# Low halves of the gated products on POOL, and scales of a unit made when both norms are known

## The chip, the cores and the metric

The kernel runs on one core of one Trainium2 chip. The metric is device time in microseconds (us) of one execution. The engines are TensorE (PE in the profile; PEld are its weight loads), VectorE (DVE), ScalarE (ACT), GpSimd (POOL) and SyncE (SP). Each engine executes its own queue of instructions in order and waits on semaphores for the others. SP issues most of the transfers; POOL issues the indirect ones.

## What is computed

Three layers in a row. `attn` is an attention over 32 memory slots for each of 4 batches and 8 heads. Its output, 2304 tokens of 512 numbers, goes through a gated layer, and that through a layer of 8 experts of which each token takes 2.

```python
# attention (4 batches, 8 heads, 576 tokens, 64 numbers, 32 slots)
a = softmax(phi, over tokens)
k_m, v_m = einsum('bhsm,bhsd->bhmd', a, k), einsum('bhsm,bhsd->bhmd', a, v)
x = softmax(q @ k_m.T / 8) @ v_m                 # -> (2304, 512)
# gated layer, d_ff = 1536
x = (sigmoid(x @ w_gate) * (x @ w_val)) @ w_out
# experts: router with noise, top 2 of 8, F = 1024
logits = x @ g + log1p(exp(x @ n)) * noise
for e in range(8):
    out[rows of e] += weight[rows of e] * (relu(x[rows of e] @ w1[e]) @ w2[e])
```

## The kernel before

Products that need more than float16 are made of two halves: a number is scaled and rounded to a float16 high half, the rest becomes a float16 low half, and a product is the sum of high-high, high-low and low-high, three matmuls into one PSUM bank. The helper `split` (L375) does it in two instructions: ScalarE writes the high half (L376), VectorE the low half (L377).

*Weights.* The matrices of the gated layer come as 64-bit patterns in 36 pieces of 512 KB, loaded by SP into four buffers (L318). Each piece is rounded to float32 in four instructions (`rounded`, L325): ScalarE scales the low words (L329), VectorE shifts and joins the high words (L331, L332), POOL adds (L333). POOL's add is the last reader of the piece, so it frees the buffer for the next load. ScalarE then sums the squares (L363 for gate and value weights, L359 for output weights), a matmul with ones (L87) sums them over the partitions, and a few VectorE instructions (L92 to L96) make a power of two and its inverse of it. The generator `weights` walks through the 18 jobs.

*Attention.* For each batch, `memory` makes the slots, `values_scale` their norm, and `attention` the weights of the tokens; POOL multiplies by the inverse sums (L278). The batch's tokens are not multiplied out: `fold` (L231) multiplies the slots into 256 columns of the gate and of the value weights (a unit u of 6) and splits the result into `wq`, with a scale `ws` (L236) made of the unit's and the batch's norms.

*Gated layer, first half.* `stage1` (L410) runs 72 times: 4 batches, 6 units, 3 chunks of 192 tokens. Twenty-four matmuls (L424) fill two PSUM banks, one for the gate and one for the value. Tanh on ScalarE (L427, with a scale `gs` made by VectorE in L388 at first use) gives `sg` in SBUF, from a ring of two buffers; VectorE writes (tanh + 1) times value back into the value's PSUM bank (L429); ScalarE takes the high half out of it (L430) and VectorE the low half (L431). PSUM has a ring of four banks for this (`pg`), which folds, attention and experts share.

*Gated layer, second half.* `stage2` (L433) multiplies 128 tokens with the output weights (L442), `tokens` splits the row and writes it out, `route` finds the two experts, and POOL scatters slot numbers (L586) after copying token numbers (L556).

*Experts.* After the last `stage1` at about 440 us, TensorE runs the experts (L764, L778) to the end; POOL gathers (L749) and scatters (L784) their rows.

*Order.* The program names the instructions in the order of the loops: in the first loop of `build`, a fold, three times a product with three steps of `weights` behind it; later products between the second halves. A planner with priorities then orders each engine's queue and adds the semaphores and the reuse of buffers. The attention of the first batch runs far ahead, that of the later ones somewhat ahead.

Of the kernel before, what the change touches and what calls it, by code (L numbers as in the profile page):

```python
# [26 lines left out]
P = 128  # L27
# [26 lines left out]
SG = 2  # L54
# [12 lines left out]
class Kern:  # L67
# [31 lines left out]
    def consts(self):  # L99
        nc = self.nc  # L100
        cp = self.cp = self.ctx.enter_context(self.tc.tile_pool(name="const", bufs=1, side="left"))
        tmp = ExitStack()
        jp = tmp.enter_context(self.tc.tile_pool(name="tmp", bufs=1, side="right")).tile([P, P], F32, name="jp")
        nc.gpsimd.iota(jp, pattern=[[1, P]], base=0, channel_multiplier=-1, allow_small_or_imprecise_dtypes=True)
        self.idf = cp.tile([P, P], F32, name="idf")
        nc.vector.tensor_scalar(self.idf, jp, 0.0, None, op0=ALU.is_equal)
        self.tri = cp.tile([P, P], F16, name="tri")
        nc.vector.tensor_scalar(self.tri, jp, 0.0, None, op0=ALU.is_gt)
        self.onef = cp.tile([P, P], F32, name="onef")
        nc.vector.memset(self.onef, 1.0)  # L110
        self.ones = cp.tile([P, P], F16, name="ones")
        nc.vector.memset(self.ones, 1.0)
        tmp.close()
# [55 lines left out]
    def memory(self, b, g):  # L169
# [21 lines left out]
        km = a2.tile([P, 2, 2, D], F32, tag="km", name="km")  # L191
# [31 lines left out]
    def values_scale(self, b):  # L223
        m = self.a2.tile([P, 1], F32, tag="vm", name="vm")
        self.xT[b] = self.xp.tile([P, 2, 2, S], F16, tag="x", name="x")
        junk = self.xT[b][:, 0, 0, :P].bitcast(BF16)
        self.nc.scalar.activation(junk, self.flat(self.vbs[b % 2]), AF.Square, accum_out=m)
        self.sv[b], iv = yield from self.norm2(self.cp, m, f"sv{b}", floor=30)
        self.invx.append(iv)

    def fold(self, b, u):  # L231
# [3 lines left out]
        s = self.cp.tile([P, 2], F32, tag="ws", bufs=4, name="ws")  # L235
        nc.vector.tensor_scalar(s, self.sw[u], self.sv[b], 2.0 ** -A_BITS, op0=ALU.mult, op1=ALU.mult)  # L236
# [12 lines left out]
    def attention(self, b):  # L249
# [4 lines left out]
        def scores(u):  # L254
# [15 lines left out]
            ex = a2.tile([P, n, M], F32, tag="ex" if u < 2 else "ex2", name="ex")  # L270
# [24 lines left out]
        self.gs[b] = {}  # L295
# [39 lines left out]
    def weights(self):  # L335
# [6 lines left out]
        def finish(u, wait):  # L342

            s, iv = yield from self.norm2(cp, sums[u], f"w{u}", wait, 2)
            self.sw.append(s)
            self.iwg.append(iv[:, 0:1])
            self.iwv.append(iv[:, 1:2])
            yield
# [36 lines left out]
    def gate_scale(self, b, u):  # L385
        if u not in self.gs[b]:
            g = self.gs[b][u] = self.cp.tile([P, 1], F32, name=f"gs{b}{u}")
            self.nc.vector.tensor_scalar(g, self.iwg[u], self.invx[b], 0.5, op0=ALU.mult, op1=ALU.mult)  # L388
        return self.gs[b][u]
# [20 lines left out]
    def stage1(self, b, u, ch):  # L410
# [16 lines left out]
        nc.scalar.activation(sg, ps[0], AF.Tanh, scale=self.gate_scale(b, u))  # L427
        pv = ps[1]
        nc.vector.scalar_tensor_tensor(pv, sg, 1.0, pv, op0=ALU.add, op1=ALU.mult)  # L429
        nc.scalar.activation(o[:, 0, :, cols], pv, AF.Copy, scale=2.0 ** -16)  # L430
        nc.vector.scalar_tensor_tensor(o[:, 1, :, cols], pv, 2.0 ** -16, o[:, 0, :, cols], op0=ALU.mult, op1=ALU.subtract)  # L431
# [45 lines left out]
    def router_consts(self):  # L477
        nc, a, cp, rz = self.nc, self.a, self.cp, self.rz
        self.ie = cp.tile([P, E], F32, name="ie")
# [417 lines left out]
    def build(self):  # L897
# [6 lines left out]
        self.snapped, self.sv, self.sw, self.wq = False, {}, [], {}  # L904
# [6 lines left out]
        self.xp, self.xT = left(mw, "xp", 2), {}  # L911
        wp = left(mraw, "w1p", 1)
        self.W = [wp.tile([P, KT, 256], F32, name=f"w{i}") for i in range(12)]
        self.gp = right(m1, "gT", GT)
        self.sp = right(m1, "sig", SG)
# [216 lines left out]
```

## Time and profile before

| | |
|---|---|
| time, median of 3 (lowest to highest) | 891.67 us (890.34 to 894.32) |
| time of the profiled execution | 891.72 us |
| its span in the trace | 889.9 us |
| PE busy | 814.8 us (92%) |
| DVE busy | 473.5 us (53%) |
| ACT busy | 456.8 us (51%) |
| POOL busy | 208.6 us (23%) |
| mean granted clock of PE | 0.973 |

The profile is of one execution. A wait "A L1 <- B L2" is time in which engine A stood before its line L1 until engine B had finished its line L2. The granted clock is a share of full speed, 1.0 being 2.4 GHz and 0.5 being 1.2 GHz. Names of tiles are those of the program without numbers.

### The profile page before, as it was taken

How to read it: one execution, taken by the hardware profiler on the slowest of the kernel's cores; microseconds unless marked ns; L12 is line 12 of the kernel's file. 1: busy time of each engine (PE TensorE's matmuls, PEld its weight loads, DVE VectorE, ACT ScalarE, POOL GpSimd, SP SyncE). 2: the span in 40 equal slices, each digit the busy share in tenths (PEclk: the TensorE clock that was granted, in tenths of full speed). 3: DMA queues.
4: the chain of work that ended last, by engine and by line, in shares of the span. 5: the costliest groups of instructions: out<-in, count | busy, mean ns of one | idle time of the engine just before them, and what ended most of it. 6: DMA issues, size and time to landing. Idle time of an engine off the chain costs nothing. (4 is left out here: it accounts for less than half of the span.)

```text
span 889.9 us, 16827 instructions
## 1 busy us (share of the span) xinstructions
PE 814.8 (92%) x6531; PEld 534.0 (60%) x6531; DVE 473.5 (53%) x1317; ACT 456.8 (51%) x907; POOL 208.6 (23%) x210
## 2 busy tenths in 40 slices
PE   5558859999999998898998999999999999999995
PEld 4347746757657765666655656665747556574752
DVE  1788788555647686874443138553444345340110
ACT  3477667615545476672323348564646446461320
POOL 1363440001110201023014443202323122332112
PEclk9998778999999999999999999999999999999998
DMA  9478639324221564546594869826565868473113
GB/s 317 151 258 292 227 115 341 132 75 102 25 78 25 166 214 142 168 166 194 145 346 107 176 132 263 200 95 143 129 188 120 166 141 214 71 117 48 25 13 47
DMA packets 126067, 135.16 MB, mean 152 GB/s; under 512 B 71968, under 2 KB 88480, under 8 KB 125472
## 3 DMA queue, kind: packets, MB, share of 16 engines
q1 hardware_dynamic: 116000, 113.30, 43.9%
q0 software_dynamic: 9984, 20.75, 12.9%
q8 instruction: 52, 0.85, 0.4%
q14 instruction: 31, 0.25, 0.1%
HBM read 87.97 MB, written 30.86 MB: 134 GB/s over the span
## 5 line engine op out<-in xcount | busy, mean ns | idle before, releaser
L424 PE MATMUL pg<-x,wq 128*128 128x192 f16 x1728 | 174.0, 258 | 23.4 <-ACT wq L376 15.1
L424 PEld LDWEIGHTS <-wq 128*128 128x128 f16 x1728 | 152.5, 103 | 44.2 <-ACT wq L376 17.7
L778 PEld LDWEIGHTS <-hT 128*128 128x128 f16 (+1 forms) x960 | 99.8, 105 | 104.8 <-DVE hT L770 0.9
L442 PE MATMUL px<-wo,gT 128*128 128x512 f16 x648 | 148.8, 379 | 0.3 <-issue 0.3
L784 POOL DMA_INDIRECT out<-y,mts x40 | 64.6, 1614 | 208.7 <-ACT y L783 206.9
L778 PE MATMUL py<-w2a,hT 128*128 128x512 f16 (+1 forms) x480 | 105.2, 379 | 0.4 <-DVE hT L770 0.4
L778 PE MATMUL py<-w2b,hT 128*128 128x512 f16 (+1 forms) x480 | 104.9, 379 | 0.0
L764 PE MATMUL ph<-xe,w1a 128*128 128x312 f16 (+2 forms) x768 | 103.3, 296 | 0.0
L770 DVE TENSOR_TENSOR hT<-r,hT 128x312 f16<-128x312 f32 (+2 forms) x128 | 57.4, 480 | 85.9 <-ACT hT L769 84.5
L764 PE MATMUL ph<-xe,w1b 128*128 128x312 f16 (+2 forms) x768 | 103.0, 296 | 0.0
L442 PEld LDWEIGHTS <-gT 128*128 128x128 f16 x648 | 61.5, 98 | 68.6 <-issue 4.5
L783 ACT ACTIVATE y<-py,css 128x512 f32<-128x512 f32 (+1 forms) x40 | 27.5, 687 | 129.6 <-PE py L778 120.6
L764 PEld LDWEIGHTS <-w1b 128*128 128x128 f16 x768 | 75.2, 98 | 27.1
L764 PEld LDWEIGHTS <-w1a 128*128 128x128 f16 x768 | 75.0, 98 | 27.1
L768 ACT ACTIVATE r<-ph 128x312 f32<-128x312 f32 (+2 forms) x128 | 49.7, 428 | 76.5 <-PE ph L764 73.0
L586 POOL DMA_INDIRECT meta<-mt,vi x36 | 36.1, 1003 | 173.8 <-DVE vi L583 46.4
L749 POOL DMA_INDIRECT xg<-xs,mts x40 | 44.4, 1110 | 87.7 <-DMA xe<-xg 49.0
L427 ACT ACTIVATE sg<-pg,gs 128x384 f32<-128x384 f32 x72 | 41.6, 578 | 41.9 <-PE pg L424 27.9
L429 DVE SCALAR_TENSOR_TENSOR pg<-sg,pg 128x384 f32<-128x384 f32 x72 | 40.2, 558 | 36.8 <-PE pg L424 25.7
L781 DVE TENSOR_TENSOR css<-mts,iw 128x1 f32<-128x1 f32 (+1 forms) x40 | 6.5, 164 | 89.5 <-ACT y L783 84.9
L430 ACT ACTIVATE gT<-pg 128x384 f16<-128x384 f32 x72 | 34.8, 485 | 36.7 <-DVE pg L429 34.4
L769 ACT CAST hT<-r 128x312 f16<-128x312 f32 (+2 forms) x128 | 53.1, 458 | 0.8
(311 smaller groups left out, 972.9 us busy)
## 6 DMA issues: line engine op xcount, KB each, us to landing
wo<-w SPq DMA_DIRECT2D x48, 512.0 KB, 5.5
st<-kv SPq DMA_DIRECT2D x16, 512.0 KB, 7.8
f<-w SPq DMA_DIRECT2D x16, 512.0 KB, 3.8
wsp<-hl SPq DMA_DIRECT2D x16, 512.0 KB, 3.5
w<-wg SPq DMA_DIRECT2D x12, 512.0 KB, 5.8
w<-wv SPq DMA_DIRECT2D x12, 512.0 KB, 4.2
w<-wo SPq DMA_DIRECT2D x12, 512.0 KB, 4.2
out<-z SPq DMA_DIRECT2D x23, 256.0 KB, 2.8
```

What stands on the lines that cost most here:

```text
L424: nc.tensor.matmul(p[:, f, :], w[:, l, g, j, f * P : (f + 1) * P], x[:, r, g, ch * QC : (ch + 1) * QC], start=n == 0, stop=n == 5)
L427: nc.scalar.activation(sg, ps[0], AF.Tanh, scale=self.gate_scale(b, u))
L429: nc.vector.scalar_tensor_tensor(pv, sg, 1.0, pv, op0=ALU.add, op1=ALU.mult)
L442: nc.tensor.matmul(p, g[:, l, f % 2, t * P : (t + 1) * P], self.wob[f // 2][:, r, f % 2, :], start=f + i == 0, stop=f == FT - 1 and i == 2)
L586: d = nc.gpsimd.indirect_dma_start(out=self.meta, out_offset=bass.IndirectOffsetOnAxis(ap=vi[:, t, k : k + 1], axis=0), in_=mt[:, t, k, :] ...
L749: self.nc.gpsimd.indirect_dma_start(out=xg.rearrange("p a b -> p (a b)"), out_offset=None, in_=self.xs[:rows, :], in_offset=bass.IndirectO ...
L764: nc.tensor.matmul(p[:, : t1 - t0], w1[:, l, k, f * P : (f + 1) * P], xe[:, x, t0:t1], start=n == 0, stop=n == 3 * KT - 1)
L768: nc.scalar.activation(r, p[:, : t1 - t0], AF.Relu, scale=2.0 ** -19)
L769: nc.scalar.copy(self.hT[:, 0, f, t0:t1], r)
L770: nc.vector.tensor_sub(self.hT[:, 1, f, t0:t1], r, self.hT[:, 0, f, t0:t1])
L778: nc.tensor.matmul(py, self.hT[:, l, f, i * P : i * P + m], w2[:, w, f, :], start=n == 0, stop=n == 3 * F2T - 1)
L784: d = nc.gpsimd.indirect_dma_start(out=self.out, out_offset=bass.IndirectOffsetOnAxis(ap=mt[:m, 0:1], axis=0), in_=y[:m], in_offset=None, ...
```

## The change

VectorE now writes (tanh + 1) times value over `sg` in SBUF instead of over the value's PSUM bank, and the high half is read from there. The low half is made by two POOL instructions instead of one on VectorE: a multiplication of `sg` by 2^-16 in place, and a subtraction of the high half. The ring of `sg` has three buffers instead of two, and its pool moves from the right to the left end of SBUF, to the pools that are closed ahead of the last block. Room is made by one buffer instead of two for `km` and for the small exponentials (`ex2`), and by building `tri` and `ones` with the router's constants.

`unit_scales` makes `ws` and `gs` for every pair of batch and unit. It is called at the end of each unit's norm and at the end of each batch's norm, and replaces the instruction in `fold` (four buffers in a ring) and `gate_scale`.

```diff
-SG = 2
+SG = 3
...
-        self.tri = cp.tile([P, P], F16, name="tri")
-        nc.vector.tensor_scalar(self.tri, jp, 0.0, None, op0=ALU.is_gt)
...
-        self.ones = cp.tile([P, P], F16, name="ones")
-        nc.vector.memset(self.ones, 1.0)
...
-        km = a2.tile([P, 2, 2, D], F32, tag="km", name="km")
+        km = self.a1.tile([P, 2, 2, D], F32, tag="km", name="km")
...
         self.invx.append(iv)
+        self.unit_scales()
 
     def fold(self, b, u):
...
-        s = self.cp.tile([P, 2], F32, tag="ws", bufs=4, name="ws")
-        nc.vector.tensor_scalar(s, self.sw[u], self.sv[b], 2.0 ** -A_BITS, op0=ALU.mult, op1=ALU.mult)
+        s = self.ws[(b, u)]
...
-            ex = a2.tile([P, n, M], F32, tag="ex" if u < 2 else "ex2", name="ex")
+            ex = (a2 if u < 2 else self.a1).tile([P, n, M], F32, tag="ex" if u < 2 else "ex2", name="ex")
...
             self.iwv.append(iv[:, 1:2])
+            self.unit_scales()
             yield
...
-    def gate_scale(self, b, u):
-        if u not in self.gs[b]:
-            g = self.gs[b][u] = self.cp.tile([P, 1], F32, name=f"gs{b}{u}")
-            self.nc.vector.tensor_scalar(g, self.iwg[u], self.invx[b], 0.5, op0=ALU.mult, op1=ALU.mult)
-        return self.gs[b][u]
+    def unit_scales(self):
+        nc = self.nc
+        for b in self.sv:
+            for u in range(len(self.sw)):
+                if (b, u) not in self.ws:
+                    s = self.ws[(b, u)] = self.cp.tile([P, 2], F32, name=f"ws{b}{u}")
+                    nc.vector.tensor_scalar(s, self.sw[u], self.sv[b], 2.0 ** -A_BITS, op0=ALU.mult, op1=ALU.mult)
+                    g = self.gs[(b, u)] = self.cp.tile([P, 1], F32, name=f"gs{b}{u}")
+                    nc.vector.tensor_scalar(g, self.iwg[u], self.invx[b], 0.5, op0=ALU.mult, op1=ALU.mult)
...
-        nc.scalar.activation(sg, ps[0], AF.Tanh, scale=self.gate_scale(b, u))
+        nc.scalar.activation(sg, ps[0], AF.Tanh, scale=self.gs[(b, u)])
         pv = ps[1]
-        nc.vector.scalar_tensor_tensor(pv, sg, 1.0, pv, op0=ALU.add, op1=ALU.mult)
-        nc.scalar.activation(o[:, 0, :, cols], pv, AF.Copy, scale=2.0 ** -16)
-        nc.vector.scalar_tensor_tensor(o[:, 1, :, cols], pv, 2.0 ** -16, o[:, 0, :, cols], op0=ALU.mult, op1=ALU.subtract)
+        nc.vector.scalar_tensor_tensor(sg, sg, 1.0, pv, op0=ALU.add, op1=ALU.mult)
+        nc.scalar.activation(o[:, 0, :, cols], sg, AF.Copy, scale=2.0 ** -16)
+        nc.gpsimd.tensor_scalar(sg, sg, 2.0 ** -16, None, op0=ALU.mult)
+        nc.gpsimd.tensor_tensor(o[:, 1, :, cols], sg, o[:, 0, :, cols], op=ALU.subtract)
...
     def router_consts(self):
         nc, a, cp, rz = self.nc, self.a, self.cp, self.rz
+        jp = rz.tile([P, P], F32, name="jpr")
+        nc.gpsimd.iota(jp, pattern=[[1, P]], base=0, channel_multiplier=-1, allow_small_or_imprecise_dtypes=True)
+        self.tri = rz.tile([P, P], F16, name="tri")
+        nc.vector.tensor_scalar(self.tri, jp, 0.0, None, op0=ALU.is_gt)
+        self.ones = rz.tile([P, P], F16, name="ones")
+        nc.vector.memset(self.ones, 1.0)
...
+        self.sp = left(mw, "sig", SG)
...
-        self.sp = right(m1, "sig", SG)
```

## Rows read from the trace of the kernel before

**Rows 1.** Stretches: length, busy us of PE, PEld, DVE, ACT, POOL; PEclk, DMA share, GB/s.

```profile
0.00:50.00 50.00, 26.78 (x192) 18.60 (x193) 24.93 (x70) 22.97 (x51) 14.99 (x21) 1.00 0.72 233
50.00:150.00 100.00, 75.76 (x831) 60.80 (x829) 83.89 (x202) 72.19 (x150) 39.54 (x51) 0.83 0.73 241
150.00:450.00 300.00, 285.23 (x2887) 195.18 (x2886) 193.52 (x637) 159.20 (x306) 40.77 (x52) 0.99 0.46 134
450.00:890.00 440.00, 427.01 (x2627) 259.46 (x2625) 171.17 (x411) 202.46 (x402) 113.28 (x86) 0.99 0.60 135
```

**Rows 2.** Waits, 50 to 150 us: us in total, times, longest us.

```profile
POOL wo L333 <- DVE wo L332: 15.2, 7, 4.4
POOL w L333 <- DVE w L332: 13.6, 6, 4.0
...
PE pg L424 <- ACT wq L376: 10.0, 6, 5.8
ACT wo L359 <- POOL wo L333: 6.4, 5, 3.5
...
PE pmx L87 <- ACT wo L363: 4.9, 2, 4.1
...
ACT wo L363 <- POOL w L333: 3.6, 5, 1.3
...
PE pg L424 <- DVE wq L377: 2.9, 5, 0.9
DVE gT L431 <- ACT gT L430: 2.4, 5, 1.0
...
PE pv L243 <- DVE gT L431: 1.8, 2, 1.0
...
ACT wq L376 <- DVE ws L236: 1.3, 2, 1.2
```

**Rows 3.** Waits of TensorE, 150 to 500 us.

```profile
PE pv L243 <- DVE wq L377: 3.2, 3, 1.7
PE pg L424 <- DVE gT L431: 2.4, 3, 1.4
```

**Rows 4.** Groups by line, whole span: busy us, mean ns, idle before, releasers.

```profile
L769 ACT CAST hT<-r 128x312 f16<-128x312 f32 (+2 forms) x128 | 53.1, 458 | 0.8
...
L431 DVE SCALAR_TENSOR_TENSOR gT<-pg,gT 128x384 f16<-128x384 f32 x72 | 39.7, 552 | 17.0 <-ACT gT L430 16.8
...
L430 ACT ACTIVATE gT<-pg 128x384 f16<-128x384 f32 x72 | 34.8, 485 | 36.7 <-DVE pg L429 34.4 <-DVE az L531 1.8 <-issue 0.4
```

**Rows 5.** Line L431 alone, 50 to 150 us: length, VectorE's busy time.

```profile
50.00:150.00 100.00, 9.77 (x18) 0.83 0.73 241
```

**Rows 6.** POOL's groups by shape, whole span.

```profile
L333 POOL TENSOR_TENSOR w<-w,w 128x512 int32<-128x512 int32 x24 | 30.9, 1293 | 39.4 <-DVE w L332 28.1 <-DVE pg L429 2.2 <-DVE psm L218 2.2
...
L278 POOL TENSOR_TENSOR ex<-ex,ssm 128x512 f32<-128x512 f32 x8 | 8.3, 1052 | 103.4 <-DVE tts L75 48.5 <-DVE ssm L276 36.0 <-DVE ssm L277 18.8
...
L278 POOL TENSOR_TENSOR ex<-ex,ssm 128x128 f32<-128x128 f32 x4 | 1.6, 401 | 23.1 <-DVE ssm L277 20.1 <-DVE sm L551 3.0
```

**Rows 7.** Waits of SP's DMA queue, 50 to 150 us.

```profile
SPq L318 <- POOL w L333: 19.4, 13, 3.2
```

**Rows 8.** Instructions of line L236: duration ns min/median/max, first and last start.

```profile
L236 DVE TENSOR_SCALAR ws<-w2s,sv0s x1: 226/226/226, 70.2 to 70.2; 128x2 f32<-128x2 f32 x1
L236 DVE TENSOR_SCALAR ws<-w3s,sv0s x1: 1273/1273/1273, 70.4 to 70.4; 128x2 f32<-128x2 f32 x1
...
L236 DVE TENSOR_SCALAR ws<-w5s,sv0s x1: 925/925/925, 129.5 to 129.5; 128x2 f32<-128x2 f32 x1
L236 DVE TENSOR_SCALAR ws<-w0s,sv1s x1: 1197/1197/1197, 130.5 to 130.5; 128x2 f32<-128x2 f32 x1
```

**Rows 9.** Instructions in order of time, 129 to 131.2 us: start, duration us.

```profile
129.12 2.52 POOL L333 TENSOR_TENSOR wo<-wo,w 128x512 int32<-128x512 int32 x2 [1.03 <-DVE wo L332]
...
130.52 0.84 ACT L376 ACTIVATE wq<-pv,ws 128x256 f16<-128x256 f32 x2 [1.15 <-DVE ws L236]
```

More of the change, by code (lines that the diff above doesn't have):

```diff
@@ L294, in turned @@
             nc.vector.scalar_tensor_tensor(ol, src, 2.0 ** A_BITS, oh, op0=ALU.mult, op1=ALU.subtract)
-        self.gs[b] = {}
         ex = {}
@@ L903, in build @@
         self.gs, self.it, self.gT, self.pxs, self.lg, self.itx, self.mt = {}, {}, {}, {}, {}, {}, {}
-        self.snapped, self.sv, self.sw, self.wq = False, {}, [], {}
+        self.snapped, self.sv, self.sw, self.wq, self.ws = False, {}, [], {}, {}
         m1, mw, mraw, wsc = self.m1, _, _, _ = ExitStack(), ExitStack(), ExitStack(), ExitStack()
```

## The prediction, made blind

> **What bounds the kernel now.** The first view is the busy time by stretch [rows 1]. Compare TensorE with the length of each stretch: it stands still for 23.2 us of the first 50, 24.2 us between 50 and 150 us, 14.8 us between 150 and 450 us, and 13.0 us after that. The last stretch is the experts' and holds no instruction of the change; the first ends before any gated product exists. What the change can move is therefore idle time in the two middle stretches, 39 us, and one thing more: between 50 and 150 us the granted clock averages 0.83, elsewhere 0.99 or 1.00. If all matmul time there scaled with the clock, its loss would be 75.76 x (1 - 0.83) = 12.9 us; that is my estimate from the row. In this stretch VectorE is the fullest engine (83.89 of 100 us), ScalarE has 72.19, and POOL 39.54.
>
> The second view is the list of waits of that stretch [rows 2]. The reader should follow it backwards. TensorE waits mostly for the first split of a folded weight on ScalarE (10.0 us) and, through the norm, for a ScalarE square (4.9 us). ScalarE executes in order, and ten times its square stands waiting for the rounding add on POOL (3.6 + 6.4 us). POOL in turn waits for VectorE's L332 (15.2 + 13.6 us). So the chain is VectorE, POOL, ScalarE, TensorE, and each link delays whatever stands behind it on the same engine. The third view, the waits of TensorE from 150 to 500 us [rows 3], shows a bound of another kind: TensorE itself, with a few short waits for VectorE.
>
> **The change part by part.** *Earlier release of PSUM.* Today the value product's bank is free after L431, in future after L429. That is one ScalarE and one VectorE instruction earlier: 485 + 552 ns [rows 4], 1.04 us. TensorE waited for L431 twice in the second stretch (1.8 us) [rows 2] and three times in the third (2.4 us, longest 1.4) [rows 3]. Cut by at most 1.04 us each, the five lose 3.8 us at the very most; some of them will find the next wait right behind. I take -3.5 us, bounds -3.8 and 0.
>
> *VectorE loses L431.* 72 instructions, 39.7 us in all [rows 4]. Eighteen of them, 9.77 us, lie in the stretch where VectorE is fullest [rows 5]; before them it also stood 2.4 us waiting for the high half [rows 2]. So VectorE is offered 12.2 us of its 100. The rest, behind 150 us, lies beside a TensorE that is 95% busy [rows 1] and is worth nothing beyond the waits already counted. How much of the 12.2 us reaches TensorE is the main unknown: the waits that VectorE feeds there are 10.0 + 4.9 + 2.9 = 17.8 us [rows 2], and they share the stretch with ScalarE and with loads. Bounds 0 and -12.2; I take rather less than a third, -3.5, because TensorE's own gaps hang on the chain through POOL and ScalarE, of which VectorE's work is one link of three.
>
> *POOL gains two instructions for each.* Nothing in the trace multiplies 128x384 on POOL. For the subtract the nearest rows are the float products: 1052 ns for 512 columns and 401 ns for 128 [rows 6], a slope of 1.70 ns a column, so 384 columns take 0.84 us; at the rate of the 512-column integer add (1293 ns) it would be 0.97. For the multiply by a constant the bounds are the 0.40 us of the 128-column product and the 0.84 us of the two-input form at its own size [rows 6]; I take 0.6, about their middle, since it has the columns of the one and half the inputs. A pair is then 1.45 us (1.24 to 1.81), 104 us over 72. In the second stretch 18 pairs put 26 us on top of 39.54 [rows 1]: POOL goes to about two thirds and is no bound by its sum. But it is in order, and the pair must wait for the high half. What is moved past are the rounding adds (behind whose buffer release the weight loads on SP's queue wait, 19.4 us in this stretch [rows 7]), the softmax products, the scatters and gathers of the router. Of the ten ScalarE waits for the rounding add, five or so end in a TensorE wait; I assume a pair stands in front of two of these: +2.9 us, bounds 0 and ten pairs, +14.5. The router's scatters come later by a pair at most, and what they feed (the first experts' rows) is needed after the last product; if that cover fails it costs 1.45 us once.
>
> *Longer life of the sigmoid buffer.* It is now held until POOL's subtract; the third buffer pays for it. After 150 us there are 54 products in 300 us, one in 5.6 us, so two spare buffers cover a POOL that is 11 us late. If POOL falls further behind, tanh waits, and with it ScalarE's queue; I price it at nothing, and it belongs to the slower rival below.
>
> *Scales made early.* The two small VectorE instructions per unit and batch are the same in number (24 + 24); they move ahead. One place pays: the scale of unit 5 starts at 129.50 us, takes 0.93 us because POOL is running its 2.52 us pair of adds, and ScalarE's split starts at 130.52 us, 1.15 us after it could have; TensorE stands 5.8 us in that gap [rows 2, 9]. All ScalarE waits on this instruction are 1.3 us [rows 2]. I take -1.2, bounds -1.3 and 0. The gap itself stays at more than 4 us, since the split still stands behind the square that waits for POOL.
>
> *The high half read from SBUF, the product written to it.* The new L429 has the sources and the target memory of the old L431 (552 ns) and costs the same. The high half's nearest row with an SBUF source is the experts' cast, 458 ns for at most 312 columns against 485 for 384 from PSUM [rows 4]; scaled to 384 columns that is 0.08 us more, 1.4 us of ScalarE in the second stretch; ScalarE has 28 us free there. Nothing. The single buffers for km and for the small softmax tile, and the two constants that are built later, are nothing as well: whole steps of attention lie between two uses, the router reads the constants long after; uncovered, each costs a small instruction once.
>
> *Clock.* Idle time in the second stretch changes by -1.5 (its share of the PSUM waits) - 1.2 - 3.5 + 2.9 = -3.3 us of 24.2, or 14%; if low-clock time shrinks along, 14% of 12.9 is -1.8. I take -1.5, bounds -12.9 and +1.5.
>
> *POOL against VectorE.* A scale instruction took 226 ns at 70.2 us and 1273 ns at 70.4; at 129.5 and 130.5 us, beside the POOL adds that ran from 129.12 to 131.64, two took 925 and 1197 ns [rows 8, 9]: the two engines block each other. More POOL time means more of that, bounds 0 and all 104 us on VectorE; behind 150 us only the short waits for VectorE's splits (3.2 us [rows 3]) would feel it: +0.5. The Trainium skill, page "SBUF — State Buffer", section "Who interferes with whom", says why: VectorE's two-port forms (copy, tensor_scalar) and forms with two SBUF inputs share one port pair with POOL, and the second to start waits for the first to end. The 1273 ns agree with it; by this rule offloading to POOL gives part of VectorE's relief back, which is the third case below.
>
> The sum: -3.5 - 3.5 + 2.9 - 1.2 - 1.5 + 0.5 = -6.3 us. Against the profiled execution's 891.72 us, which is the median's 891.67 within 0.1, that is 885.4.
>
> **The rivals.** (a) *POOL becomes the link that sets the weight chain* (slower). Place: the rounding adds between 50 and 131 us. If a pair stands ahead of each of the ten adds on which ScalarE waited, the chain grows by 14.5 us; against it stand 8.2 us (PSUM, relief, scales) and the clock gives nothing: 891.7 + 14.5 - 8.2 + 0.5 = 898.5. It decides as soon as more than six of the ten are hit (9.2 / 1.45). For it: POOL's adds come in bursts just where TensorE's gaps are [rows 9]. Against: POOL idles 60 us of that stretch, and 28.8 of these waiting for VectorE, which gets faster.
> (b) *The relief does not arrive* (no change). Of nine scale instructions between 50 and 150 us, three took 0.7 to 1.05 us longer than an undisturbed one [rows 8]. That is 0.3 us an instruction with POOL 40% busy, 0.5 at two thirds; on some 40 small VectorE instructions of this kind it eats 8 of 9.8 us. Left are PSUM and half the scales against POOL's delay: -3.5 - 0.6 + 2.9 = 890.5. The rule quoted above points here.
> (c) *The gaps close and the clock stays up* (much faster). Half of the 17.8 us of waits go, and with 8.9 / 24.2 of the idle time as much of the clock's loss, 4.7; with PSUM and POOL's delay: 891.7 - 8.9 - 4.7 - 3.5 + 2.9 = 877.5.
> (d) *The scales are not early*: the planner that orders each engine's queue leaves them behind the same L332. Then only that term goes, 886.6.
>
> **How the numbers follow.** Chances: forecast 0.43, (a) 0.17, (b) 0.26, (c) 0.11, (d) 0.03. 0.5%, about what a measurement of this kernel can tell from no change, is 4.5 us, so faster means below 887.2. About 0.07 of the forecast's own spread (880 to 890) lies above that; (c), (d) and the rest lie below: faster 0.50. (b) and that part make the same: 0.33. (a): 0.17. The range runs from the near side of (c) to just short of (a)'s time, 876 to 897: it leaves out some of both ends, less than 2 in 10.
>
> **What would show each step.** The release: no TensorE wait that names L431's successor on POOL, and fewer that name L429. The relief: VectorE near 75 of 100 us between 50 and 150, and TensorE's idle time there near 21. POOL's price: the two new lines at 0.6 and 0.85 us, and ScalarE's waits for L333 no longer than 13 us. The scales: 0.2 us instructions right behind the norms, none between 128 and 131. The forecast falls if tanh waits for POOL's subtract (the buffers), if ScalarE's waits for L333 double (a), or if VectorE's busy time hardly falls (b).

## The result, and the profile after

Forecast: 885.4 us and faster. Measured: 901.65 us in the median of four runs, the kernel before 892.38 us beside them, a ratio of 1.0128 [1.0079, 1.0178]. On two other chips the changed kernel took 1.0103 [1.0053, 1.0152] and 1.0174 [1.0138, 1.0211] times the time before. So the sign was wrong, and the time lies 4.7 us above the upper end of the range. The kernel before spreads over some 7 to 13 us on one chip when it is executed nine times or more, so below the verdict goes by ratios (time over that of the kernel before on the same chip, with a 95% interval), and single traces only say where.

The profiled execution of the changed kernel took 898.4 us, its span 896.6. Its stretches, in the columns of [rows 1]:

```profile
50.00:150.00 100.00, 74.03 (x789) 60.68 (x795) 67.00 (x167) 65.02 (x136) 71.73 (x85) 0.76 0.63 202
150.00:450.00 300.00, 282.94 (x2906) 194.41 (x2891) 186.05 (x585) 165.75 (x315) 161.95 (x160) 0.99 0.47 134
```

From 50 to 150 us VectorE falls from 83.89 to 67.00 us, further than the 9.77 us that were taken from it; a part of that is work that moved out of the stretch (in the first 50 us VectorE has 29.03 us in this trace, 24.93 before). POOL rises from 39.54 to 71.73 and is now nearly as full as TensorE. And TensorE's idle time, which was to shrink to 21 us, grows from 24.2 to 26.0. The freight moved, and nothing came of it at the engine that sets the end. The two new groups on POOL, and the waits of the same stretch (against [rows 2, 7]; the line numbers are those of the changed kernel, in which L328 is the rounding add, L355 and L359 the squares, L313 the weight loads):

```profile
L431 POOL TENSOR_SCALAR sg<-sg 128x384 f32<-128x384 f32 x72 | 90.1, 1252 | 121.8 <-ACT gT L430 121.5
L432 POOL TENSOR_TENSOR gT<-sg,gT 128x384 f16<-128x384 f32 x72 | 69.5, 965 | 5.3
```

```profile
POOL sg L431 <- ACT gT L430: 15.8, 8, 7.9
POOL w L328 <- DVE w L327: 4.5, 3, 3.0
...
ACT wo L355 <- POOL wo L328: 8.5, 5, 3.1
ACT wo L359 <- POOL w L328: 5.8, 4, 2.2
...
PE pg L424 <- ACT wq L372: 16.1, 8, 4.0
...
SPq L313 <- POOL wo L328: 30.7, 8, 9.2
SPq L313 <- POOL w L328: 21.6, 11, 5.1
```

Three things are to be seen. A pair takes 1.25 + 0.97 = 2.22 us, not 1.45. POOL's adds wait 4.5 us for VectorE's step just ahead of them (L327, the L332 of before) instead of 28.8 [rows 2]: VectorE is early now, and POOL itself is what is late. And the loads of the weights' ring on SP's queue, which may start only when POOL's add has freed a buffer, wait 52.3 us. Before it was the 19.4 us of [rows 7] and this line beside it, 38.6 in all:

```profile
SPq L318 <- POOL wo L333: 19.2, 8, 5.4
```

At the end of the weights POOL's order of time shows it full (start, duration):

```profile
126.38 1.30 POOL L328 TENSOR_TENSOR wo<-wo,w 128x512 int32<-128x512 int32 x1 [3.19 <-DVE psm L215]
127.64 1.18 POOL L431 TENSOR_SCALAR sg<-sg 128x384 f32<-128x384 f32 x1
128.77 1.31 POOL L328 TENSOR_TENSOR wo<-wo,w 128x512 int32<-128x512 int32 x1
130.04 0.92 POOL L432 TENSOR_TENSOR gT<-sg,gT 128x384 f16<-128x384 f32 x1
130.91 1.29 POOL L328 TENSOR_TENSOR wo<-wo,w 128x512 int32<-128x512 int32 x1
132.17 1.16 POOL L431 TENSOR_SCALAR sg<-sg 128x384 f32<-128x384 f32 x1
133.42 0.92 POOL L432 TENSOR_TENSOR gT<-sg,gT 128x384 f16<-128x384 f32 x1
134.29 1.28 POOL L328 TENSOR_TENSOR wo<-wo,w 128x512 int32<-128x512 int32 x1
135.53 1.17 POOL L431 TENSOR_SCALAR sg<-sg 128x384 f32<-128x384 f32 x1
136.79 0.91 POOL L432 TENSOR_TENSOR gT<-sg,gT 128x384 f16<-128x384 f32 x1
137.66 1.28 POOL L328 TENSOR_TENSOR wo<-wo,w 128x512 int32<-128x512 int32 x1
```

Hardly a gap from 126 to 139 us, and something of a pair directly in front of each of the last four adds. In [rows 9] the last two adds ran as one block of 2.52 us, over at 131.64; here the last ends at 138.94, 7.3 us later. But not all of this came up here. Both kernels make the 36 adds one for one. The three before those of [rows 9], in the kernel before:

```profile
119.46 1.29 POOL L333 TENSOR_TENSOR wo<-wo,w 128x512 int32<-128x512 int32 x1 [0.55 <-DVE wo L332]
125.11 1.29 POOL L333 TENSOR_TENSOR wo<-wo,w 128x512 int32<-128x512 int32 x1 [4.35 <-DVE wo L332]
126.82 1.28 POOL L333 TENSOR_TENSOR wo<-wo,w 128x512 int32<-128x512 int32 x1 [0.41 <-DVE wo L332]
```

So the last five adds of the changed kernel start 6.9, 3.7, 4.1, 5.2 and 7.3 us later than these and the two of [rows 9]: half of the lateness of the last comes up among the last four, the rest is older. That begins at 102 us:

```profile
100.55 1.28 POOL L328 TENSOR_TENSOR wo<-wo,w 128x512 int32<-128x512 int32 x1
109.72 1.17 POOL L431 TENSOR_SCALAR sg<-sg 128x384 f32<-128x384 f32 x1 [7.89 <-ACT gT L430]
110.97 0.91 POOL L432 TENSOR_TENSOR gT<-sg,gT 128x384 f16<-128x384 f32 x1
111.85 1.29 POOL L328 TENSOR_TENSOR wo<-wo,w 128x512 int32<-128x512 int32 x1
```

The add at 100.55 is 0.4 us ahead of its counterpart (100.96), the next is 8.0 us behind its own (103.81). POOL stood 7.89 us before the multiply until the high half was there. The add behind it could not have gone much earlier, though: VectorE's step for it ended at 110.27, so the pair held it for 1.6 us. Why the whole chain stood there is not shown.

### The profile page after: what moved, and what is told of

Same layout as the page of the kernel before. It is cut to its first block, busy times and chain, and to the rows that moved or that the text cites. A ratio compares the mean times of both kernels' runs of the same rounds, so it can differ in the third digit from the quotient of the medians.

```text
span 896.6 us, 16924 instructions
## 1 busy us (share of the span) xinstructions
PE 812.1 (91%) x6531; PEld 532.0 (59%) x6531; DVE 454.8 (51%) x1245; ACT 459.3 (51%) x907; POOL 365.9 (41%) x355
## 4 chain that ended last, share of the span: by engine, by line
PE 69%; DVE 9%; ACT 7%; DMA 6%; POOL 4%; issue 4%; SPq 0%; POOLq 0%; ACTq 0%; DVEq 0%
PE py L785 23%; PE ph L771 22%; PE px L443 10%; PE pg L424 9%; DMA xt<-row 3%; PE pa L261 2%; PE pv L239 1%; PE pa L186 1%; POOL sg L431 1%; DVE wq L373 1%; DVE sg L429 1%; DMA wsp<-hl 1%; ACT sg L427 1%; DMA w<-wo 1%; DVE wo L373 1%
## 5 line engine op out<-in xcount | busy, mean ns | idle before, releaser
L424 PE MATMUL pg<-x,wq 128*128 128x192 f16 x1728 | 176.7, 260 | 32.1 <-ACT wq L372 19.9
L431 POOL TENSOR_SCALAR sg<-sg 128x384 f32<-128x384 f32 x72 | 90.1, 1252 | 121.8 <-ACT gT L430 121.5
L756 POOL DMA_INDIRECT xg<-xs,mts x40 | 42.3, 1058 | 87.0 <-DMA xe<-xg 51.5
L432 POOL TENSOR_TENSOR gT<-sg,gT 128x384 f16<-128x384 f32 x72 | 69.5, 965 | 5.3
L429 DVE SCALAR_TENSOR_TENSOR sg<-sg,pg 128x384 f32<-128x384 f32 x72 | 39.6, 550 | 45.4 <-PE pg L424 32.5
L430 ACT ACTIVATE gT<-sg 128x384 f16<-128x384 f32 x72 | 37.3, 519 | 35.4 <-DVE sg L429 33.8
L373 DVE SCALAR_TENSOR_TENSOR wq<-pv,ws,wq 128x256 f16<-128x256 f32 x96 | 43.0, 478 | 23.6 <-ACT wq L372 19.6
```

The costliest lines, as they stand in the source:

```text
L373: self.nc.vector.scalar_tensor_tensor(lo, src, sc, hi, op0=ALU.mult, op1=ALU.subtract)
L424: nc.tensor.matmul(p[:, f, :], w[:, l, g, j, f * P : (f + 1) * P], x[:, r, g, ch * QC : (ch + 1) * QC], start=n == 0, stop=n == 5)
L429: nc.vector.scalar_tensor_tensor(sg, sg, 1.0, pv, op0=ALU.add, op1=ALU.mult)
L431: nc.gpsimd.tensor_scalar(sg, sg, 2.0 ** -16, None, op0=ALU.mult)
L432: nc.gpsimd.tensor_tensor(o[:, 1, :, cols], sg, o[:, 0, :, cols], op=ALU.subtract)
```

## The experiments

Where a time is given without a ratio it is the median on that chip.

**One part undone, or moved to half of the products.** e1 gives the low half back to VectorE (from SBUF, one instruction); e2 does so for the first 24 products only, e3 for the other 48 only.

```diff
-        nc.gpsimd.tensor_scalar(sg, sg, 2.0 ** -16, None, op0=ALU.mult)
-        nc.gpsimd.tensor_tensor(o[:, 1, :, cols], sg, o[:, 0, :, cols], op=ALU.subtract)
+        nc.vector.scalar_tensor_tensor(o[:, 1, :, cols], sg, 2.0 ** -16, o[:, 0, :, cols], op0=ALU.mult, op1=ALU.subtract)
```

> The changed kernel with one edit: VectorE makes the low half again, in one instruction, from the product in SBUF; POOL does none of it. Scales, third buffer, places in SBUF and the earlier release of PSUM stay. If POOL's place in the weight chain made the loss (chain), the loss goes and the PSUM release and the scales are left: 886 to 891 us, last rounding add near 130 us. If the scales or the layout made it, 897 to 903 us stay.

> The changed kernel, but the first 24 of the 72 products (batch 0 and the first chunk of batch 1, made beside the weights) have their low half on VectorE; the other 48 keep POOL. Chain: the loss lies in the first 24, so this is 887 to 892 us, like e1. If POOL work takes VectorE's time wherever it is (port), two thirds of the loss stay: 896 to 899.

> The reverse of e2: POOL makes the low half of the first 24 products, VectorE that of the other 48. Chain: the whole loss, 897 to 904 us, and the last rounding add near 137 us as in the changed kernel. Port: a third of the loss, 893 to 896.

Measured, with 886.26 us before on that chip: e1 890.75 us, 1.0037 [1.0015, 1.006]; e2 (POOL late) 895.59, 1.0108 [1.0074, 1.0143]; e3 (POOL early) 896.08, 1.0094 [1.0063, 1.0125]. Most of the loss is the low half on POOL, and both places cost: the theory that only the weights' stretch matters falls with e2, the theory that only the later stretch matters with e3. In medians e1 loses 4.5 us, e2 9.3 and e3 9.8. If the costs add, all pairs on POOL would lose 9.3 + 9.8 - 4.5 = 14.6 us, 1.0165, which lies among the ratios of the whole change; on this chip the whole change was not run.

**The rest of the change, in two parts.** e4b is the changed kernel with products and low halves as before; e8 is the kernel before with the product written to SBUF (and its two buffers of `sg`). The early scales without the new layout were not measured. e14 is e4b once more, on another chip.

```diff
-        nc.vector.scalar_tensor_tensor(pv, sg, 1.0, pv, op0=ALU.add, op1=ALU.mult)
-        nc.scalar.activation(o[:, 0, :, cols], pv, AF.Copy, scale=2.0 ** -16)
+        nc.vector.scalar_tensor_tensor(sg, sg, 1.0, pv, op0=ALU.add, op1=ALU.mult)
+        nc.scalar.activation(o[:, 0, :, cols], sg, AF.Copy, scale=2.0 ** -16)
```

> The changed kernel, with the products and their low halves as in the kernel before (product in PSUM, low half by VectorE): only the scales made early, the moved tiles, the third gate buffer and the router's constants at the start of the router's part are left. The kernel with the low half back on VectorE from SBUF was 1.0037 times the kernel before [1.0015, 1.006]. Theory 'scales and constants cost': this kernel shows the same 1.002 to 1.006. Theory 'the product in SBUF costs': this kernel lies within 0.2 per cent of the kernel before, and the kernel with only the product moved shows the loss.

> The kernel before, with one edit: the gated product is written over the gate's tile in SBUF, and ScalarE's and VectorE's halves are read from there; POOL gets nothing, scales and constants stay where they were. Theory of the forecast: PSUM's tiles come free about 1.8 us earlier, worth up to 3.5 us, so 0.996 to 1.000 times the kernel before. Theory 'the product in SBUF costs' (two gate tiles only, which now wait for the low half, and an extra SBUF read that meets POOL's port): 1.002 to 1.006. If both this kernel and the one with only scales and layout lie within 0.2 per cent of the kernel before, the 0.37 per cent of both together is a matter of order, not of either part.

> The changed kernel with the products and low halves as before, once more and in more rounds, as a version that may beat both kernels: it had 0.9959 [0.9928, 0.999]. If the early scales are worth what the forecast gave them and the clock (1 to 3 us), the ratio lies at 0.995 to 0.999 and its interval leaves out 1; if the first result was the spread of a few executions, it lies at 0.999 to 1.003.

Measured: e4b 0.9959 [0.9928, 0.999], e14 0.9987 [0.9963, 1.0011], e8 1.0004 [0.9978, 1.003]. Scales and layout together are a gain of 0 to 0.4 per cent, the product in SBUF is nothing that can be told from none; neither explains the 1.0037 [1.0015, 1.006] of e1, which has both and the low half on VectorE. That stays open. No version clearly beats the kernel before.

**The constants.** The trace of after has VectorE's triangle waiting 3.5 us for POOL's iota at 139 us, and TensorE idle for 3.3 us behind it. e7 makes the triangle without POOL (a running sum over the identity) and takes the numbers from POOL at the start; e7b makes it at the start, as the kernel before does. a0 is the changed kernel itself beside e7.

```diff
-        nc.gpsimd.iota(jp, pattern=[[1, P]], base=0, channel_multiplier=-1, allow_small_or_imprecise_dtypes=True)
+        nc.vector.tensor_tensor_scan(jp, self.onef, self.idf, 0.0, op0=ALU.mult, op1=ALU.add)
...
-        nc.vector.tensor_scalar(self.tri, jp, 0.0, None, op0=ALU.is_gt)
+        nc.vector.tensor_tensor(self.tri, jp, self.idf, op=ALU.subtract)
```

> The changed kernel itself, so that its parts can be set against it on one chip. All theories expect what was measured: 1.008 to 1.018 times the kernel before. It also gives a second trace, in which POOL's two instructions should again take 1.25 and 0.97 us, VectorE's step for the triangle should again wait for POOL's iota near 139 us, and TensorE should stand idle for about 3 us there.

> The changed kernel, with the router's constants no longer made by POOL at 139 us: the triangle is made by VectorE alone (a running sum over the identity, minus the identity), and the expert and token numbers come from POOL in the first microseconds. Theory 'constants behind POOL': the 3.5 us wait of the triangle's step for POOL's iota, which held the first split of a folded weight and left TensorE idle from 136.8 to 140.0 us, is gone and not given back, so this kernel ends 2 to 4 us before the changed kernel on the same chip. Rival: the split then waits for the next late thing on VectorE (the rounding of the last weights behind POOL, or the fold), TensorE's pause stays, and the gain is under 1 us.

> The changed kernel, with the triangle and the ones made at the start of the program and kept from there, as in the kernel before; the scales lie in one tile, so that they fit beside it. In the run without POOL's iota the wait of 3.2 us stayed and was then for the last rounding add: the constants lie in memory that the weights' ring leaves, so their first write waits for the last reader of that memory, which is POOL. Here VectorE writes nothing there. Theory 'memory of the ring': VectorE's wait of 3.2 to 3.5 us near 139 us goes and the kernel gains 2 to 4 us on the changed kernel, 1.005 to 1.010 times the kernel before. Rival: ScalarE's square of the last weight waits 3.1 us for the same add, in front of the splits of the fold in ScalarE's queue, so the splits come no earlier and the gain is under 1.5 us, 1.009 to 1.014.

Measured: a0 1.0103 [1.0053, 1.0152], e7 1.0142 [1.0095, 1.0188], e7b 1.0165 [1.0124, 1.0206]. No gain. The trace of e7 shows why the first idea was wrong; VectorE and ScalarE at 142 us, in order of time:

```profile
142.75 0.42 DVE L485 TENSOR_TENSOR_SCAN jpr<-onef,idf 128x128 f32<-128x128 f32 x1 [3.19 <-POOL wo L332]
...
142.75 1.15 ACT L359 ACTIVATE wo<-wo,w5i 128x1024 bf16<-128x1024 f32 x1 [3.15 <-POOL wo L332]
```

Without the iota the same wait is for POOL's last rounding add (the tile lies in the memory that the ring leaves), and ScalarE waits at the same moment for the same add, in front of the splits that TensorE needs. The iota was the last thing named, not the cause.

**The pair later in POOL's order.** e6 issues the pair of a product one product later, behind the next weights' steps.

```diff
+        self.lows.append(lower)
...
                 turns(weights, weights, weights)
+                self.lower(1)
```

> The changed kernel, with POOL's two instructions of a product issued one product later in the first loop, behind the rounding adds of three weight steps; from product 24 on nothing differs. Theory 'order on POOL': POOL takes its queue in order, and a pair that waits for its own product (7.9 us before the pair at 109.7 us in the changed kernel) holds rounding adds whose data is there; with the pairs a product later the adds come earlier, the last add starts 3 to 6 us earlier than in the changed kernel, and the time falls by about as much, to 1.004 to 1.008 times the kernel before. Rival 'length on POOL': the pairs cost their 2.2 us wherever they stand, since POOL is busy without a gap towards the end of the weights; the last add starts within 1.5 us of where it did and the time stays at 1.009 to 1.014.

Measured: 1.019 [1.0135, 1.0244]. The trace has the same order on POOL as the changed kernel (pair at 109.1 and 110.4 us, add at 111.2, and so on to the last add at 136.9): the planner, which orders each engine's queue, put the pair back. So this run says nothing about order.

**How much on POOL, and of which kind.** e5b drops the subtraction; e12 has one two-input instruction alone; e13 one multiply that waits for the high half; e11 two multiplies, the first in place as in the changed kernel; e15 the full pair for every second product, VectorE for the others. e5b, e11, e12 and e13 leave the true low halves out of the computation. a1 and b0 are the two kernels themselves on e15's chip.

```diff
 e5b
+        nc.gpsimd.tensor_scalar(o[:, 1, :, cols], sg, 2.0 ** -30, None, op0=ALU.mult)
 e12
+        nc.gpsimd.tensor_tensor(o[:, 1, :, cols], sg, sg, op=ALU.subtract)
 e13
+        nc.gpsimd.tensor_scalar(o[:, 1, :, cols], o[:, 0, :, cols], 2.0 ** -12, None, op0=ALU.mult)
 e11
+        nc.gpsimd.tensor_scalar(sg, sg, 2.0 ** -16, None, op0=ALU.mult)
+        nc.gpsimd.tensor_scalar(o[:, 1, :, cols], sg, 2.0 ** -14, None, op0=ALU.mult)
 e15
+        if (ch + u) % 2:
+            nc.vector.scalar_tensor_tensor(o[:, 1, :, cols], sg, 2.0 ** -16, o[:, 0, :, cols], op0=ALU.mult, op1=ALU.subtract)
```

> The changed kernel, with POOL's subtraction left out: one instruction of POOL makes something of the low half's size and type from the product alone (the low halves of the gated products are left out of the computation). 0.97 us of the 2.22 us of each pair go. Theory 'length on POOL': the loss, 9 to 13 us, shrinks in proportion, by 4 to 6 us: 1.004 to 1.009 times the kernel before. Theory 'order on POOL': the multiply still stands ahead of the adds and waits for its product, so the loss shrinks by 1 to 2 us only: 1.009 to 1.013. Theory 'VectorE and POOL in each other's way': VectorE's busy time from 150 to 450 us falls by about half of the 20 us that it was given back, to some 175 us.

> The changed kernel, with POOL's second instruction, the subtraction of two tiles, replaced by another multiply of one tile by a constant (the low halves are left out of the computation). POOL still has two instructions for each product, the first still waits for ScalarE's high half, and together they are longer (1.17 and 1.17 us alone). Without the subtraction altogether the loss was gone (0.9974). Theory 'length on POOL': the loss is back, 1.010 to 1.018 times the kernel before, and the last rounding add starts near 138 us. Theory 'a two-input instruction of POOL holds VectorE' (in the run of single instructions VectorE's low half took 1.34 us beside POOL's subtraction, against 0.55 us in this kernel): with one-input instructions alone the loss stays away, 0.996 to 1.003, and VectorE's busy time from 150 to 450 us is near 171 to 176 us, not 186. Theory 'waiting for the high half on POOL's queue': the loss is back too, and the next run, whose one instruction waits alike, shows it as well.

> The changed kernel, with one instruction on POOL for each product, and that one with two inputs: the product minus itself, written as the low half, which is so left out (zero). It waits for VectorE's product only and takes 0.9 to 1.0 us, 1.2 us less than the pair. Theory 'a two-input instruction holds VectorE': most of the loss stays, 1.006 to 1.013 times the kernel before, VectorE's busy time from 150 to 450 us near 180 to 186 us. Theories 'length on POOL' and 'waiting for the high half': none of it stays, 0.995 to 1.001.

> The changed kernel, with one instruction on POOL for each product, a multiply by a constant that reads the high half (the low half is left out). It takes about 1.2 us like the one of the run without the subtraction, but it has to wait for ScalarE's high half, as both instructions of the changed kernel do. Theory 'waiting for the high half on POOL's queue': the loss is back, at least half of it, 1.005 to 1.013 times the kernel before, and POOL's waits from 50 to 150 us name the high half with 15 us or more. Theories 'length on POOL' and 'two-input instruction': as without the subtraction, 0.995 to 1.001.

> The changed kernel, with the low half of every second product on VectorE (one instruction from SBUF) and of the others on POOL, as a pair: POOL's added time is 1.1 us for each product on the mean, as in the runs with one instruction, but every pair is as long as in the changed kernel. Theory 'a point from which length decides': POOL has gaps enough for that, and the loss is gone, 0.995 to 1.002 times the kernel before. Theory 'in proportion': each pair costs the same, and half the loss of 1.0 to 1.6 per cent stays, 1.005 to 1.009.

> The changed kernel once more, for a comparison on this chip with the kernel that has every second pair: 1.008 to 1.018 times the kernel before. Product 24 should again start 7 to 10 us later than in the kernel before.

> The kernel before, for its trace on the same chip as the two others. Its product 24 should start near 200 us; if it starts near 208 us here, the place of the loss read from traces of different chips was wrong.

POOL's groups of e5b, e12 and e13, and then the two of e11:

```profile
L431 POOL TENSOR_SCALAR gT<-sg 128x384 f16<-128x384 f32 x72 | 87.2, 1212 | 179.8 <-DVE sg L429 138.2 <-DVE ssm L272 6.5 <-DVE mf L550 6.3
```

```profile
L431 POOL TENSOR_TENSOR gT<-sg 128x384 f16<-128x384 f32 x72 | 61.5, 856 | 199.4 <-DVE sg L429 155.1 <-DVE mf L550 6.9 <-DVE ssm L272 6.8
```

```profile
L431 POOL TENSOR_SCALAR gT<-gT 128x384 f16<-128x384 f16 x72 | 89.4, 1242 | 167.9 <-ACT gT L430 163.8 <-PE pk L577 2.0
```

```profile
L431 POOL TENSOR_SCALAR sg<-sg 128x384 f32<-128x384 f32 x72 | 89.6, 1246 | 104.0 <-ACT gT L430 101.4 <-PE pk L578 0.7
L432 POOL TENSOR_SCALAR gT<-sg 128x384 f16<-128x384 f32 x72 | 85.2, 1183 | 5.9
```

The ring's waits from 50 to 150 us (SP's queue for POOL's add) in b0, then in a1, then in e11:

```profile
SPq L318 <- POOL w L333: 21.9, 14, 3.2
SPq L318 <- POOL wo L333: 18.8, 8, 5.3
```

```profile
SPq L313 <- POOL wo L328: 29.1, 8, 8.6
SPq L313 <- POOL w L328: 23.5, 13, 5.1
```

```profile
SPq L313 <- POOL wo L328: 30.9, 8, 8.8
SPq L313 <- POOL w L328: 25.3, 13, 5.8
```

And the start of product 24 (counted from 0; the first of the second loop of products), as its tanh in the order of time, in b0 and then in a1:

```profile
200.17 0.58 ACT L427 ACTIVATE sg<-pg,gs 128x384 f32<-128x384 f32 x1 [1.81 <-PE pg L424]
```

```profile
211.43 0.58 ACT L427 ACTIVATE sg<-pg,gs 128x384 f32<-128x384 f32 x1 [0.50 <-PE pg L424]
```

The same readings of all of them, in the order of POOL's time for a product (all times in us; the last column is the span less the start of product 24). b0, e15 and a1 ran on one chip, e14, e12, e13 and e11 on a second, e5b on a third, and the last three rows, the versions with one part undone, on a fourth. The last column is to be read within one chip only: the kernel before has 683.3 there in b0 and 689.4 in the trace of [rows 1], while its product 24 starts at 200.2 and 200.5.

| kernel | POOL for a product | ratio | ring's waits | product 24 at | from there |
|---|---|---|---|---|---|
| b0 (before) | 0 | 1 | 40.7 | 200.2 | 683.3 |
| e14 | 0 | 0.9987 [0.9963, 1.0011] | 42.5 | 199.5 | 684.9 |
| e12 | 0.86 | 0.9997 [0.9974, 1.0021] | 40.3 | 197.8 | 681.6 |
| e5b | 1.21 | 0.9974 [0.9947, 1.0001] | 45.0 | 202.1 | 684.9 |
| e13 | 1.24 | 0.9993 [0.9966, 1.002] | 47.1 | 205.7 | 679.6 |
| e15 | 2.22 for every second | 1.0095 [1.0064, 1.0127] | 44.5 | 202.8 | 684.3 |
| a1 (after) | 2.22 | 1.0174 [1.0138, 1.0211] | 52.6 | 211.4 | 689.5 |
| e11 | 2.43 | 1.017 [1.0134, 1.0206] | 56.2 | 213.1 | 687.3 |
| e1 | 0 | 1.0037 [1.0015, 1.006] | 41.7 | 202.4 | 683.0 |
| e2 | 2.22 for the last 48 products | 1.0108 [1.0074, 1.0143] | 41.6 | 202.1 | 687.7 |
| e3 | 2.18 for the first 24 products | 1.0094 [1.0063, 1.0125] | 53.0 | 208.7 | 682.2 |

What follows. POOL's time for one product is the cause: e11 has no two-input instruction, more POOL time, and the whole loss. Having two inputs is not (e12), and a single instruction that waits for the high half is free as well (e13). Nor is the loss in proportion to POOL's time: 0.9 to 1.2 us a product are free, 2.2 to 2.4 cost 1 to 1.7 per cent. The costly ones are all two instructions and the free ones all one; but the second follows the first almost without a gap (5.3 us over 72 pairs), and one instruction of 2.2 us was not tried. Nor does the sum over the run seem to decide: e15 has on the mean about as much POOL time as e13 and half of a1's loss. That fits a cost of each long stay in front of something that waits. It does not show it, since e15 also has half of its low halves on VectorE from SBUF, and with all of them there e1 lost 0.37 per cent without POOL.

Where it is lost, e1, e2 and e3 show on one chip. Pairs for the first 24 products alone (e3) raise the ring's waits from 41.7 to 53.0 us and start product 24 6.3 us later; late pairs alone (e2) change neither, and lose 4.7 us behind it. (The three traces are of executions 3 to 4 us faster than the medians of their kernels.) In a1 against b0 product 24 is 11.3 us later and the ring's waits are 11.9 us longer: the adds free their buffers later, the weights are loaded later, and what hangs on the last weights starts later. In the table product 24 moves with the ring's waits from row to row, which is an association over eleven traces; the ring was not changed by itself. It moves as closely with the last add, which starts 68 to 71.5 us earlier in all of these traces (at 130.2 us in b0, 140.0 in a1, 144.1 in e11), so whether the ring or what else waits for the adds makes it late is open. And being late at product 24 is not yet a loss: e13 is 6.1 us behind e14 there, on the same chip, and makes up 5.3 us of it afterwards, which is not explained.

The clock alone does not make product 24 late. From 50 to 150 us its mean is 0.79 in e1 and in e11, of which one starts product 24 at 202.4 and the other at 213.1 us:

```profile
50.00:150.00 100.00, 76.78 (x816) 61.03 (x815) 79.47 (x191) 69.80 (x144) 38.77 (x51) 0.79 0.68 220
50.00:150.00 100.00, 66.37 (x692) 53.45 (x693) 66.90 (x170) 62.81 (x133) 74.43 (x82) 0.79 0.59 190
```

Behind product 24 a1 loses 6.2 us more. Its trace shows tanh standing for POOL's subtraction, twice, at the last products:

```profile
420.17 0.58 ACT L427 ACTIVATE sg<-pg,gs 128x384 f32<-128x384 f32 x1 [2.71 <-POOL gT L432]
435.04 0.58 ACT L427 ACTIVATE sg<-pg,gs 128x384 f32<-128x384 f32 x1 [2.46 <-POOL gT L432]
```

and the last transposed row keeps TensorE waiting for 3.13 us instead of 0.35. That fits e2's loss with late pairs alone; these two waits were not taken away by themselves. It is not in every pair of traces: from product 24 on, the first trace of the changed kernel takes 688.7 us, and that of [rows 1] 689.4. The trace of e15 is of its fastest execution (888.9 us, the median is 892.6) and shows little of its loss, so where e15 loses is open too.

**Single instructions.** m1 measures POOL's forms, each three times, with VectorE's beside them.

> Computes none of the reference; it measures single instructions, nothing beside them: on POOL a multiply by a constant over 128x384 float32 in place, to another tile, to float16 and over 128 columns, and a subtraction and a product of two tiles of the same size; on VectorE a multiply and the one instruction of the low half. If the 1.17 us of the multiply is the instruction's own price, it is 1.1 to 1.2 us here too, and over 128 columns about a third of that; if it came from writing in place or from VectorE's work beside it, the form to another tile, or all of them, take 0.9 us or less, no more than the subtraction of two tiles.

In order of time, POOL and VectorE:

```profile
14.13 1.16 POOL L38 TENSOR_SCALAR r1t<-r1t 128x384 f16<-128x384 f32 x1
15.27 0.99 POOL L40 TENSOR_TENSOR r1t<-r1t,r1t 128x384 f32<-128x384 f32 x1
15.33 1.34 DVE L48 SCALAR_TENSOR_TENSOR r1t<-r1t,r1t 128x384 f16<-128x384 f32 x1 [4.51 <-POOL r1t L38]
...
18.34 0.50 POOL L31 COPY r2t<-x 128x384 f32<-128x384 f32 x1
18.92 1.17 POOL L32 TENSOR_SCALAR r2t<-r2t 128x384 f32<-128x384 f32 x1
```

The 1.17 us of the multiply are its own price, in place or not, to float32 or float16. Over 128 columns it takes 0.52. The copy of the same tile takes 0.50, the two-input subtraction 0.99.

## Why the prediction was wrong, step by step

**POOL's price, the term that failed first.** The subtraction was put at 0.84 us and took 0.97, the upper of its two bounds. The multiply was put at 0.6 with 0.84 as its upper bound, and took 1.25. The bound was no bound: it rested on the argument that one input costs less than two, and no row of before said so. The pair left its range (1.24 to 1.81) at 2.22. The term of which it is the price stood at +2.9 us; e2 and e3 put the low half on POOL at 4.8 and 5.3 us beyond e1.

**The number of hits.** I let two of ten adds have a pair in front. In the order of time above, all of the last four have all or half of one; from 50 us on it is 14 of 25 adds that follow such an instruction without a wait. ScalarE's waits for the add came to 8.5 + 5.8 = 14.3 us against 10.0 [rows 2], over the 13 that the forecast had set as its limit. The order is not independent of the load: as POOL fills, each add queues behind what came while the one before it ran. With 2.22 us rival (a) would have decided from more than four adds on (9.2 / 2.22), not from more than six. Rival (a), POOL as the link that sets the weight chain, had the right engine and the right place for the larger part of the loss, and was given 0.17. That its 898.5 us meet the 898.4 of the profiled execution (median 901.65) is luck: it reckoned with a pair of 1.45 us in front of all ten adds and with 8.2 us of gains, of which the runs show at most the scales' part; its sign, ScalarE's waits for the add doubled, did not come; and it had no loss in the later products.

**A wait that was read and not priced.** The forecast named the weight loads on SP's queue as standing behind the adds [rows 7], quoted half of that wait, and gave it no term. Of the waits for POOL's add it grew most, by 13.7 us, and the lateness of product 24 goes with it.

**VectorE's relief** (-3.5). It came at VectorE in the stretch of the weights, and POOL's adds all but stopped waiting for it. The chain of the forecast (VectorE, POOL, ScalarE, TensorE) was right; the step that failed was to credit the first link's gain and the second link's loss side by side. Here the later of the two counted: POOL's inputs were mostly early, and POOL was late.

**Release of PSUM** (-3.5). The waits of TensorE's matmuls for L431 are gone from the trace, and none names POOL's successor, as foretold; one weight load does, for 0.7 us, and one matmul after 150 us now waits 1.4 us for L429, for which none waited before. By itself the release is worth nothing measurable (e8, with two buffers of `sg`: 1.0004 [0.9978, 1.003]; 3.5 us would have been 0.9961).

**Scales** (-1.2). They came early: the one of unit 5 at 106.1 us took 220 ns, and none stands near 130 us. e4b (0.9959 [0.9928, 0.999]) and e14 (0.9987 [0.9963, 1.0011]), which hold the layout as well, agree with a gain of this size, and do not tell it from none.

**Clock** (-1.5). It went the other way, 0.76 instead of 0.83 from 50 to 150 us. Two slices of the changed kernel (TensorE's busy time, instructions, granted clock):

```profile
90.00:100.00 10.00, 4.87 (x68) 0.77 0.81 275
100.00:110.00 10.00, 9.48 (x56) 0.55 0.54 165
```

TensorE stands for half of the first, and in the second runs mostly at the lower of its two levels (1.2 of 2.4 GHz): 56 matmuls fill 9.48 us. In the kernel before the slice from 100 us has 0.80. A pause that is followed by a lower clock costs twice; how much of the loss that is was not separated by an experiment.

**POOL against VectorE** (+0.5, and rival (b)). The relief is in part given back: of the 39.7 us taken from VectorE its total fell by 18.7 only (473.5 to 454.8). But that is not the loss: e11 gave back less (447.1 in total) and lost as much. By lines, most of what was given back lies on the small instructions of the router; TensorE's waits for the one that it needs there (`o`) are 3.2 us from 150 to 500 us, against 2.3 before.

**The third buffer and the constants, at nothing.** The constants were right in their effect, although a wait of 3.5 us names them. The buffer was not quite: tanh stood 5.2 us in a1.

## What to carry to other kernels

Before work is moved to an engine that executes in order, list everything that waits for that engine, DMA queues that wait for its buffers included, and price each new instruction as a delay of each of them; the engine's mean load says little, since one stay of 1.2 us was free here and one of 2.2 us was not. Where two links of one chain change in opposite ways, do not add the gain and the loss: here the later link set the time. And a wait's named releaser is the last thing that came: take it away in an experiment before believing in it.

## What the chip showed beyond that

A multiply by a constant on POOL takes longer than a two-input subtraction of the same size, 1.17 against 0.99 us for 384 columns, and more than twice a copy (0.50). The Trainium skill, page "GPSIMD Engine Reference", section "4.1 Engine selection", calls one-input work there roughly line-rate; the copy may be read so, the multiply disagrees, and the measurement decides.

VectorE's low half with all operands in SBUF took 1.34 us when it began 0.06 us after a two-input subtraction on POOL, against 0.55 us for the same instruction from PSUM [rows 4] and 0.56 in the median from SBUF in e1; it ended 0.41 us after POOL's did. The Trainium skill, page "SBUF — State Buffer", section "Who interferes with whom", says that a VectorE instruction with two SBUF inputs contends with a POOL instruction that reads SBUF; the row agrees. In e11, which has no two-input instruction on POOL for the products, VectorE is less busy, and the kernel no faster.
